# Gated linear attention and a rational MLP on one core: one activation table set, head pairs padded to 64 rows, x kept on chip, MLP steps 2048 wide

## The chip, the cores and the metric

The program runs on one core of one Trainium2 chip. The metric is the device time of one execution in microseconds (us). Engines are named as in the profile: PE is TensorE (PEld its weight loads), DVE VectorE, ACT ScalarE, POOL GpSimd, SP the queue that issues most of the DMAs.

## What is computed

Four batches, 8 heads, 768 steps, head dimension 48; then an MLP over the 3072 tokens with 384 inputs, 2048 hidden units and 384 outputs. Inputs are float32, the output is float32.

```python
f = 1.0 / (1.0 + np.exp(-f_logit))
for t in range(S):
    state = f[:, :, t, :, None] * state + np.einsum('bhd,bhe->bhde', k[:, :, t], v[:, :, t])
    y[:, :, t] = np.einsum('bhd,bhde->bhe', q[:, :, t], state)
x = y.transpose(0, 2, 1, 3).reshape(B * S, H * D)
h = x @ w_in
P = a[0] + a[1] * h + a[2] * h**2 + a[3] * h**3
Q = 1.0 + abs(b[0]) * abs(h) + abs(b[1]) * h**2
out = (P / (Q + 1e-06)) @ w_out
```

## The kernel before

The 768 steps are cut into NC = 6 chunks of C = 128. For each chunk the attention is done in two head groups of four heads, each tile holding 4 heads x 4 batches x 48 = 768 columns on 128 partitions (the steps). ACT takes the log of the gate in two steps, `sig` (Sigmoid, L113) and `lsig` (Ln, L115); PE sums it along the chunk with a triangular matrix (`csT`, L119); ACT takes exp of that sum and of its negative (L123, L125); DVE scales q (L128), POOL scales k (L130). Then, head by head: 8 transposes into `psB` (L139, L141) and two DVE copies out; scores `sc_ps` and their masking on DVE (L160, L165); `y_ps`, for each batch one matmul with the values and one with the running state (L169, L173); ACT copies `y_ps` out and SP writes it to a DRAM tensor `xT_bridge` (L179); the state is updated (L184 to L192).

The MLP of the chunk reads `xT_bridge` back (`xc`), so that its 512 tokens lie in columns. It goes through KF = 16 tiles of 128 hidden units, each 512 wide: three matmuls (`h_ps`, L203), a DVE copy to bf16 (`hb`, L207), then a chain of steps over DVE, ACT and POOL. The division is exp(-ln(Q)): `lnQ` (L226) and `Qinv` (L228) on ACT. The product goes into `gall`; when all 16 tiles are there, four groups of 16 matmuls of 384 columns each (`o_ps`, L233), one for each batch, give the output, which ACT copies out (L237).

The order on each engine is not written by hand: a scheduler interleaves the independent work of the next chunk's attention with the MLP of this one, within the limits of the pools' buffers (most PSUM pools have one buffer).

## Time and profile before

| what | value |
|---|---|
| median of 3 runs | 821.11 us (818.91 to 821.45) |
| the profiled execution's span, first to last instruction | 820.2 us |
| that execution's own time beside its span | not given apart; the median of the runs is 0.9 us above this span |
| ACT busy | 629.0 us, 77% |
| PE busy, DVE busy, POOL busy | 424.6, 386.7, 160.4 us |

The busy share is an average over stages with different limits. The timeline shows when each instruction began and how long it took; two instructions that follow each other on one engine can overlap a little, so their starts are closer than their durations. "granted clock" is PE's clock in shares of 2.4 GHz.

### The profile page before, as it was taken

To read this page: it belongs to the slowest core of one execution; us is meant where nothing else is said; L and a number is where in the kernel's file an instruction comes from. 1 tells how busy PE (TensorE), PEld (TensorE's weight loads), DVE (VectorE), ACT (ScalarE), POOL (GpSimd) and SP (SyncE) were. 2 spreads that over 40 slices of the span, in tenths; PEclk is the share of its full clock that TensorE was granted. 3 is DMA by queue.
4 is the path that set the end of the run, shared out by engine and by line. 5 is a ranking of instruction groups with operands and counts; after the bars stand their busy time and mean duration, and the time that the engine had idled before them with its cause. 6 is when DMAs were issued, how large, how long until landed. Compare 5 with 4: busy or idle time off the path is not lost. (4 is left out here: it accounts for less than half of the span.)

```text
span 820.2 us, 6861 instructions
## 1 busy us (share of the span) xinstructions
PE 424.6 (52%) x2052; PEld 185.2 (23%) x2052; DVE 386.7 (47%) x838; ACT 629.0 (77%) x780; POOL 160.4 (20%) x174
## 2 busy tenths in 40 slices
PE   0198743339923528954527843336964335643325
PEld 0055310015500104511104510003620002300002
DVE  0054554642646642665652545553555543255550
ACT  0577599994699993699993399995169996199992
POOL 3233211310312210223210221131012220021120
PEclk9999999999555557655557555556655555655557
DMA  9997530205601401412101300002100000100001
GB/s 160 152 126 86 97 58 0 13 5 125 90 0 20 49 2 36 64 24 26 26 2 38 36 9 0 0 0 34 43 14 1 0 0 19 42 0 0 0 0 40
DMA packets 127110, 29.55 MB, mean 36 GB/s; under 512 B 121569, under 2 KB 126689, under 8 KB 127073
## 3 DMA queue, kind: packets, MB, share of 16 engines
...
q14 instruction: 22, 0.17, 0.1%
...
## 5 line engine op out<-in xcount | busy, mean ns | idle before, releaser
L233 PE MATMUL o_ps<-w_out_sb,gall 128*128 128x384 bf16 x384 | 109.9, 409 | 214.2 <-DVE gall L229 211.9
L203 PE MATMUL h_ps<-xc,w_in_sb 128*128 128x512 bf16 x288 | 139.4, 612 | 98.7 <-DVE hb L207 92.5
L216 POOL TENSOR_SCALAR pB<-hb,a_sb 128x512 bf16<-128x512 bf16 x96 | 97.6, 1017 | 424.9 <-DVE hb L207 409.1
L229 DVE TENSOR_TENSOR gall<-Pp,Qinv 128x512 bf16<-128x512 bf16 x96 | 44.4, 463 | 178.2 <-ACT Qinv L228 178.2
L226 ACT ACT_TABLE_LOAD x95 | 121.9, 1283 | 1.7
L233 PEld LDWEIGHTS <-gall 128*128 128x128 bf16 x384 | 40.9, 109 | 315.9 <-DVE gall L229 286.2
L228 ACT ACT_TABLE_LOAD x85 | 109.1, 1283 | 1.5
L223 DVE SCALAR_TENSOR_TENSOR u<-h,babs,habs 128x512 bf16<-128x512 bf16 x96 | 73.0, 761 | 34.4 <-ACT habs L211 34.2
L178 ACT CAST y_sb<-y_ps 48x512 bf16<-48x512 f32 x48 | 27.7, 576 | 67.7 <-PE y_ps L173 65.3
L207 DVE CAST hb<-h_ps 128x512 bf16<-128x512 f32 x96 | 65.8, 686 | 25.2 <-PE h_ps L203 25.1
L213 ACT ACTIVATE pA<-hb,a_sb 128x512 bf16<-128x512 bf16 x96 | 77.0, 802 | 0.0
L211 ACT ACTIVATE habs<-hb,babs 128x512 bf16<-128x512 bf16 x96 | 68.1, 709 | 7.2 <-DVE hb L207 7.1
L226 ACT ACTIVATE lnQ<-u,one_eps 128x512 bf16<-128x512 bf16 x96 | 69.4, 723 | 1.1
L203 PEld LDWEIGHTS <-w_in_sb 128*128 128x128 bf16 x288 | 34.5, 124 | 154.6 <-issue 152.7
L228 ACT ACTIVATE Qinv<-lnQ 128x512 bf16<-128x512 bf16 x96 | 60.5, 630 | 0.9
L237 ACT COPY o_sb<-o_ps 128x384 f32<-128x384 f32 x24 | 11.5, 479 | 64.8 <-PE o_ps L233 63.4
L107 POOL DMA_DIRECT2D vn<-in_v_dram x48 | 36.5, 775 | 122.7 <-PE y_ps L173 109.9
L169 PE MATMUL y_ps<-sc_sb,vn 128*48 128x128 bf16 x192 | 54.1, 282 | 3.8 <-DVE sc_sb L165 2.7
L173 PE MATMUL y_ps<-qt_d,state 48*48 48x128 bf16 x192 | 54.1, 282 | 0.0
L192 DVE TENSOR_TENSOR state<-stmp,alast 48x192 bf16<-48x192 f32 x48 | 21.2, 442 | 61.2 <-PE y_ps L173 61.2
L165 DVE TENSOR_TENSOR sc_sb<-sc_ps,mask 128x512 bf16<-128x512 f32 x48 | 33.0, 688 | 33.4 <-PE sc_ps L160 33.1
L219 DVE TENSOR_TENSOR t<-pA,h 128x512 bf16<-128x512 bf16 x96 | 40.3, 420 | 17.7 <-ACT pA L213 17.7
...
## 6 DMA issues: line engine op xcount, KB each, us to landing
...
```

The lines of the kernel that those rows point to most:

```text
L169: nc.tensor.matmul(y_ps[:, b * C:(b + 1) * C], vn[:, jo + b * D:jo + (b + 1) * D], sc_sb[:, b * C:(b + 1) * C], start=True, stop=False)
L173: nc.tensor.matmul(y_ps[:, b * C:(b + 1) * C], state[:, b * D:(b + 1) * D], qt_d[:, b * C:(b + 1) * C], start=False, stop=True)
L203: nc.tensor.matmul(h_ps, w_in_sb[:, kk, m * P:(m + 1) * P], xc[:, kk].rearrange("p b s -> p (b s)"), start=(kk == 0), stop=(kk == KD - 1))
L207: nc.vector.tensor_copy(hb, h_ps)
L211: nc.scalar.activation(habs, hb, AF.Abs, scale=babs[:, 0:1])
L213: nc.scalar.activation(pA, hb, AF.Identity, scale=a_sb[:, 3:4], bias=a_sb[:, 2:3])
L216: nc.gpsimd.tensor_scalar(pB, hb, a_sb[:, 1:2], a_sb[:, 0:1], op0=ALU.mult, op1=ALU.add)
L223: nc.vector.scalar_tensor_tensor(u, h2, babs[:, 1:2], habs, op0=ALU.mult, op1=ALU.add)
L226: nc.scalar.activation(lnQ, u, AF.Ln, bias=one_eps)
L228: nc.scalar.activation(Qinv, lnQ, AF.Exp, scale=-1.0)
L229: nc.vector.tensor_mul(gall[:, m, :], Pp, Qinv)
L233: nc.tensor.matmul(o_ps, gall[:, mm, sub * C:(sub + 1) * C], w_out_sb[:, mm, :], start=(mm == 0), stop=(mm == KF - 1))
```

## The change

The kernel is written anew around the same chunks of 128 steps.

- One activation table set is loaded at the start (L45). The gate's log becomes ln(1 + exp(-f)), so that all functions on ACT are Exp, Ln, Abs and copies.
- A unit of attention is now (chunk c, batch pair u): two batches, all 8 heads, 768 columns. Twelve units. Heads lie in pairs, each padded from 48 to 64, so that one transpose turns two heads (16 transposes of 128 x 128 a unit, L151) and the state of two heads lies on 128 partitions. The zeros of the padding are written once into three rotating buffers (L60 to L66). POOL computes nothing; it only issues the loads of v and the weights.
- y comes out with steps on partitions and is transposed on PE into `xT` in SBUF (L219 to L225). There is no DRAM bridge and no read back.
- The MLP goes in 4 groups of 4 hidden tiles, each step 2048 wide. ACT copies the matmul result to bf16 (`hy`, two pieces of 1024, L240); |h| is a bitwise AND on DVE (`z`); the polynomial is evaluated on DVE in bf16 by five `tensor_scalar` steps (TENSOR_SCALAR, one tensor input; L243, L245, L253, L255, L257) and four products of two tensors (L246, L254, L256, L258); ACT keeps Ln (`lq`) and Exp (`qi`).
- Loads run three units ahead; the first unit's loads stand ahead of the weights.
- PSUM: `ps2` and `ps1`, one buffer each, are shared by tag: `cs`, `sc` and `y` take turns in one, `tp`, `sv` and `xps` in the other. `hp` has two buffers, `op` one.

```diff
...
+    nc.scalar.preload_act_table_set("natural_log_exp_and_others")
...
+    for i in range(NQK):
+        t = consts.tile([C, UB, 2, H, 64], BF16, name=f"qkp{i}")
+        nc.vector.memset(t.rearrange("p a b c d -> p (a b c d)").bitcast(F32), 0.0)
+        qkp.append(t)
+        t = consts.tile([C, UB, H, 64], BF16, name=f"lsp{i}")
+        nc.vector.memset(t.rearrange("p b c d -> p (b c d)").bitcast(F32), 0.0)
+        lsp.append(t)
...
+    def load(c, u):
+        t0 = c * C
+        fn = ld.tile([C, UB, H, D], F32, name="fn")
+        kn = ld.tile([C, UB, H, D], F32, name="kn")
+        qn = ld.tile([C, UB, H, D], F32, name="qn")
+        vn = ld.tile([C, UB, H, D], BF16, name="vn")
+        for j in range(UB):
+            b = u * UB + j
+            for dst, src, eng in ((fn, f_logit, nc.sync), (kn, k, nc.sync),
+                                  (qn, q, nc.sync), (vn, v, nc.gpsimd)):
+                eng.dma_start(out=dst[:, j],
+                              in_=src[b, :, t0:t0 + C, :].rearrange("h t d -> t h d"))
+        loaded[c, u] = (fn, kn, qn, vn)
...
-            sig = sb.tile([C, GD], F32, tag="sig")
-            nc.scalar.activation(sig, fn, AF.Sigmoid)
-            lsig = bf.tile([C, GD], BF16, tag="lsig")
-            nc.scalar.activation(lsig, sig, AF.Ln)
...
-            AT = hsb.tile([C, GD], F32, tag="AT")
-            nc.scalar.activation(AT, csT, AF.Exp, scale=1.0)
-            AinvT = hsb.tile([C, GD], F32, tag="AinvT")
-            nc.scalar.activation(AinvT, csT, AF.Exp, scale=-1.0)
-            qt_n = bf.tile([C, GD], BF16, tag="qt_n")
-            nc.vector.tensor_mul(qt_n, qn, AT)
-            kt_n = bf.tile([C, GD], BF16, tag="kt_n")
-            nc.gpsimd.tensor_mul(kt_n, kn, AinvT)
...
+        ef = at.tile([C, UB, H, D], F32, name="ef")
+        nc.scalar.activation(ef.rearrange(fl), fn.rearrange(fl), AF.Exp, scale=-1.0)
+        nc.scalar.activation(ls[:, :, :, 0:D], ef, AF.Ln, bias=1.0)
+        cs = ps2.tile([C, 2, 512], F32, name="cs", tag="w2")
+        for j in range(UB):
+            nc.tensor.matmul(cs[:, j, 0:DM].rearrange("p (h d) -> p h d", h=H), U, ls[:, j, :, 0:D],
+                             start=True, stop=True)
+        A = at.tile([C, UB, H, D], F32, name="A")
+        Ai = at.tile([C, UB, H, D], F32, name="Ai")
+        nc.scalar.activation(A.rearrange("p b h d -> p b (h d)"), cs[:, :, 0:DM], AF.Exp, scale=-1.0)
+        nc.scalar.activation(Ai.rearrange("p b h d -> p b (h d)"), cs[:, :, 0:DM], AF.Exp, scale=1.0)
+        nc.vector.tensor_mul(qk[:, :, 0, :, 0:D], qn, A)
+        nc.vector.tensor_mul(qk[:, :, 1, :, 0:D], kn, Ai)
...
+        for j in range(UB):
+            tp = ps1.tile([P, 2, HP, C], BF16, name="tp", tag="w1")
+            for i in range(2):
+                for p in range(HP):
+                    nc.tensor.transpose(tp[:, i, p, :],
+                                        qk[:, j, i, 2 * p:2 * p + 2, :].rearrange("t h d -> t (h d)"),
+                                        ident)
+            t = at.tile([P, 2, HP, C], BF16, name="qkT", bufs=4)
+            nc.scalar.copy(t.rearrange("p a b c -> p (a b c)"), tp.rearrange("p a b c -> p (a b c)"))
...
+            sv = ps1.tile([P, 512], F32, name="sv", tag="w1")
+            svv = sv[:, 0:UB * HP * D].rearrange("p (b h e) -> p b h e", b=UB, h=HP)
+            al = sv[:, 448:448 + UB * HP]
+            for j in range(UB):
+                for p in range(HP):
+                    nc.tensor.matmul(al[:, j * HP + p:j * HP + p + 1],
+                                     ls[:, j, 2 * p:2 * p + 2, :].rearrange("t h d -> t (h d)"),
+                                     ones, start=True, stop=True)
+                    for i in range(2):
+                        h = 2 * p + i
+                        nc.tensor.matmul(svv[64 * i:64 * i + 64, j, p, :],
+                                         qk[:, j, 1, h, :], vn[:, j, h, :],
+                                         start=True, stop=True)
+        scm = []
+        for j in range(UB):
+            sc = ps2.tile([C, 2, HP, C], F32, name="sc", tag="w2")
+            for p in range(HP):
+                for i in range(2):
+                    r = slice(64 * i, 64 * i + D)
+                    nc.tensor.matmul(sc[:, i, p, :], qkT[j][r, 1, p, :], qkT[j][r, 0, p, :],
+                                     start=True, stop=True)
+            m = at.tile([C, 2 * HP, C], BF16, name="scm", bufs=4)
+            mb = bass.AP(tensor=mask.tensor, offset=mask.offset,
+                         ap=[mask.ap[0], [0, 2 * HP], mask.ap[1]])
+            nc.vector.tensor_mul(m, sc.rearrange("s i p t -> s (i p) t"), mb)
...
-                nc.scalar.copy(y_sb, y_ps)
-                nc.sync.dma_start(
-                    out=xT[h * D:(h + 1) * D, :].rearrange("d (b s) -> d b s", b=B)[:, :, t0:t0 + C],
-                    in_=y_sb.rearrange("d (b c) -> d b c", b=B))
...
+        y = ps2.tile([C, 2, 512], F32, name="y", tag="w2")
+        yv = y[:, :, 0:UB * HP * D].rearrange("t i (b p e) -> t i b p e", b=UB, p=HP)
+        for j in range(UB):
+            for p in range(HP):
+                for i in range(2):
+                    h = 2 * p + i
+                    nc.tensor.matmul(yv[:, i, j, p, :], scm[j][:, i * HP + p, :], vn[:, j, h, :],
+                                     start=True, stop=(c == 0))
+                    if c > 0:
+                        r = slice(64 * i, 64 * i + D)
+                        nc.tensor.matmul(yv[:, i, j, p, :], qkT[j][r, 0, p, :], st[r, j, p, :],
+                                         start=False, stop=True)
+        ysb = at.tile([C, UB, HP, 2, D], BF16, name="ysb")
+        for i in range(2):
+            nc.scalar.copy(ysb[:, :, :, i, :].rearrange("t b p e -> t (b p) e"),
+                           yv[:, i].rearrange("t b p e -> t (b p) e"))
+        if c < NC - 1:
+            alast = at.tile([P, UB * HP], F32, name="alast")
+            nc.scalar.activation(alast, al, AF.Exp, scale=-1.0)
+            ab = bass.AP(tensor=alast.tensor, offset=alast.offset,
+                         ap=[alast.ap[0], alast.ap[1], [0, D]])
+            stv = st.rearrange("p b h e -> p (b h) e")
+            svf = svv.rearrange("p b h e -> p (b h) e")
+            if c == 0:
+                nc.vector.tensor_mul(stv, svf, ab)
+            else:
+                stmp = at.tile([P, UB * HP, D], F32, name="stmp")
+                nc.vector.tensor_add(stmp, svf, stv)
+                nc.vector.tensor_mul(stv, stmp, ab)
+        for j in range(UB):
+            b = u * UB + j
+            xps = ps1.tile([P, KD, C], BF16, name="xps", tag="w1")
+            yf = ysb[:, j].rearrange("t p i e -> t (p i e)")
+            for kk in range(KD):
+                nc.tensor.transpose(xps[:, kk, :], yf[:, kk * P:(kk + 1) * P], ident)
+            nc.scalar.copy(xT[:, :, b * C:(b + 1) * C], xps)
...
-        xc = msb.tile([P, KD, B, C], BF16, tag="xc")
-        for kk in range(KD):
-            nc.sync.dma_start(out=xc[:, kk],
-                              in_=xT.rearrange("d (b s) -> d b s", b=B)[kk * P:(kk + 1) * P, :, t0:t0 + C])
...
-            nc.vector.tensor_copy(hb, h_ps)
-            h2 = msb.tile([P, NT], BF16, tag="h2")
-            nc.vector.tensor_mul(h2, hb, hb)
-            habs = msb.tile([P, NT], BF16, tag="habs")
-            nc.scalar.activation(habs, hb, AF.Abs, scale=babs[:, 0:1])
-            pA = msb.tile([P, NT], BF16, tag="pA")
-            nc.scalar.activation(pA, hb, AF.Identity, scale=a_sb[:, 3:4],
-                                 bias=a_sb[:, 2:3])
-            pB = msb.tile([P, NT], BF16, tag="pB")
-            nc.gpsimd.tensor_scalar(pB, hb, a_sb[:, 1:2], a_sb[:, 0:1],
-                                    op0=ALU.mult, op1=ALU.add)
-            t1 = msb.tile([P, NT], BF16, tag="t1")
-            nc.vector.tensor_mul(t1, pA, h2)
-            Pp = msb.tile([P, NT], BF16, tag="Pp")
-            nc.vector.tensor_add(Pp, t1, pB)
-            u = msb.tile([P, NT], BF16, tag="u")
-            nc.vector.scalar_tensor_tensor(u, h2, babs[:, 1:2], habs,
-                                           op0=ALU.mult, op1=ALU.add)
-            lnQ = msb.tile([P, NT], BF16, tag="lnQ")
-            nc.scalar.activation(lnQ, u, AF.Ln, bias=one_eps)
-            Qinv = msb.tile([P, NT], BF16, tag="Qinv")
-            nc.scalar.activation(Qinv, lnQ, AF.Exp, scale=-1.0)
-            nc.vector.tensor_mul(gall[:, m, :], Pp, Qinv)
...
+        gall = gp.tile([P, KF, NT], BF16, name="gall")
+        W = G * NT
+        for g in range(KF // G):
+            y = ms.tile([P, W], BF16, name="hy")
+            for hh in range(G // 2):
+                hp = psh.tile([P, 2, NT], F32, name="hp")
+                for e in range(2):
+                    m = g * G + hh * 2 + e
+                    for kk in range(KD):
+                        nc.tensor.matmul(hp[:, e, :], w_in_sb[:, kk, m * P:(m + 1) * P], xT[:, kk, :],
+                                         start=(kk == 0), stop=(kk == KD - 1))
+                nc.scalar.copy(y[:, hh * 2 * NT:(hh + 1) * 2 * NT], hp.rearrange("p a n -> p (a n)"))
+            z = ms.tile([P, W], BF16, name="z", bufs=1)
+            nc.vector.tensor_scalar(z.bitcast(U16), y.bitcast(U16), 0x7FFF, None, op0=ALU.bitwise_and)
+            w = ms.tile([P, W], BF16, name="w")
+            nc.vector.tensor_scalar(w, z, babs[:, 1:2], babs[:, 0:1], op0=ALU.mult, op1=ALU.add)
+            nc.vector.tensor_mul(w, w, z)
+            lq = ms.tile([P, W], F32, name="lq", bufs=1)
+            nc.scalar.activation(lq, w, AF.Ln, bias=one_eps)
+            qi = ms.tile([P, W], BF16, name="qi")
+            nc.scalar.activation(qi, lq, AF.Exp, scale=-1.0)
+            t = ms.tile([P, W], BF16, name="t")
+            nc.vector.tensor_scalar(t, y, a_sb[:, 3:4], a_sb[:, 2:3], op0=ALU.mult, op1=ALU.add)
+            nc.vector.tensor_mul(t, t, y)
+            nc.vector.tensor_scalar(t, t, a_sb[:, 1:2], None, op0=ALU.add)
+            nc.vector.tensor_mul(t, t, y)
+            nc.vector.tensor_scalar(t, t, a_sb[:, 0:1], None, op0=ALU.add)
+            nc.vector.tensor_mul(gall[:, g * G:(g + 1) * G, :].rearrange("p a n -> p (a n)"), t, qi)
+        for b in range(B):
+            op = pso.tile([P, DM], F32, name="op")
+            for mm in range(KF):
+                nc.tensor.matmul(op, gall[:, mm, b * C:(b + 1) * C], w_out_sb[:, mm, :],
+                                 start=(mm == 0), stop=(mm == KF - 1))
+            osb = ms.tile([P, DM], F32, name="osb")
+            nc.scalar.copy(osb, op)
+            nc.sync.dma_start(out=out[b * S + c * C:b * S + (c + 1) * C, :], in_=osb)
...
+    AHEAD = 3
+    for x in order[:1]:
+        load(*x)
+    load_weights()
+    for x in order[1:AHEAD]:
+        load(*x)
+    nxt = AHEAD
+    for c in range(NC):
+        xT = xp.tile([P, KD, NT], BF16, name="xT")
+        for u in range(NU):
+            if nxt < len(order):
+                load(*order[nxt])
+                nxt += 1
+            attention(c, u, xT)
+        mlp(c, xT)
```

ACT, in the MLP of a chunk before: `lnQ` and `Qinv` are Ln and Exp of one tile of 512 columns, `habs` and `pA` belong to its neighbours.

```order
L228 ACT_TABLE_LOAD
L228 ACTIVATE Qinv<-lnQ 128x512
L226 ACT_TABLE_LOAD
L226 ACTIVATE lnQ<-u,one_eps 128x512
L211 ACTIVATE habs<-hb,babs 128x512
L228 ACT_TABLE_LOAD
L228 ACTIVATE Qinv<-lnQ 128x512
L213 ACTIVATE pA<-hb,a_sb 128x512
```

ACT, in the MLP of chunk 1 after the change: `hy` are the copies out of `hp`, `lq` and `qi` Ln and Exp of a group, and `qkT` the copy of the next chunk's transposed q and k.

```order
L240 CAST hy<-hp 128x1024 [waits PE_49] x2
L240 CAST hy<-hp 128x1024 [waits DVE_49,PE_49]
L240 CAST hy<-hp 128x1024 [waits PE_49]
L248 ACTIVATE lq<-w,one_eps 128x2048 [waits DVE_49]
L155 COPY qkT<-tp 128x1024 [waits PE_49]
L250 ACTIVATE qi<-lq 128x2048 [waits Activation_49]
L240 CAST hy<-hp 128x1024 [waits DVE_49]
L248 ACTIVATE lq<-w,one_eps 128x2048 [waits DVE_49,Activation_49]
L240 CAST hy<-hp 128x1024
L250 ACTIVATE qi<-lq 128x2048 [waits Activation_49]
```

The table loads are gone from between Ln and Exp, the copies of the second group stand ahead of the first group's Ln, and a copy that waits for PE (`qkT`) stands between the first group's Ln and Exp.

DVE, in the same place after the change: the first 12 steps of the MLP of chunk 1, groups one and two in turn.

```order
L243 TENSOR_SCALAR z<-hy 128x2048
L253 TENSOR_SCALAR t<-hy,a_sb 128x2048
L245 TENSOR_SCALAR w<-z,babs 128x2048
L254 TENSOR_TENSOR t<-t,hy 128x2048
L246 TENSOR_TENSOR w<-w,z 128x2048
L255 TENSOR_SCALAR t<-t,a_sb 128x2048
L243 TENSOR_SCALAR z<-hy 128x2048
L256 TENSOR_TENSOR t<-t,hy 128x2048
L245 TENSOR_SCALAR w<-z,babs 128x2048
L257 TENSOR_SCALAR t<-t,a_sb 128x2048
L246 TENSOR_TENSOR w<-w,z 128x2048
L258 TENSOR_TENSOR gall<-t,qi 128x2048
```

Before, DVE took seven steps of 512 for each of the 16 tiles, with ACT's `habs` and `pA` and POOL's `pB` between them; now nine steps of 2048 for each of 4 groups, and only `hy` and `qi` come from another engine.

DVE, at the end of the same MLP: the last group's steps and those of the next chunk's first attention unit (`scm`, `stmp`, `state`), up to the second unit's q.

```order
L258 TENSOR_TENSOR gall<-t,qi 128x2048 [waits DVE_49,Activation_49]
L254 TENSOR_TENSOR t<-t,hy 128x2048 [waits DVE_49]
L185 TENSOR_TENSOR scm<-sc,mask 128x1024 [waits PE_49]
L255 TENSOR_SCALAR t<-t,a_sb 128x2048 [waits DVE_49]
L216 TENSOR_TENSOR stmp<-sv,state_85 128x384 [waits Activation_49]
L256 TENSOR_TENSOR t<-t,hy 128x2048 [waits DVE_49]
L217 TENSOR_TENSOR state_85<-stmp,alast 128x384 [waits DVE_49,PE_49]
L257 TENSOR_SCALAR t<-t,a_sb 128x2048 [waits DVE_49]
L258 TENSOR_TENSOR gall<-t,qi 128x2048 [waits DVE_49,Activation_49]
L143 TENSOR_TENSOR qkp_81<-qn,A 128x2x8x48 [waits DMAHW5_49,DMAHW2_49,Activation_49]
```

Before, the state of one head was updated between tiles of 512. Now the state update of a unit, which waits for PE to have read the old state in the `y` matmuls, stands ahead of the last two steps of the MLP's last group.

## Rows read from the trace of the kernel before

**Rows 1.** The page, busy time, share of the span and instructions of the engines.

```profile
PE 424.6 (52%) x2052; PEld 185.2 (23%) x2052; DVE 386.7 (47%) x838; ACT 629.0 (77%) x780; POOL 160.4 (20%) x174
```

**Rows 2.** The page, the chain of work that ended last, by engine.

```profile
ACT 20%; PE 7%; issue 1%; DVE 1%; DMA 1%; ACTq 0%; SPq 0%
```

**Rows 3.** Timeline in one MLP: start, duration, engine, line, instruction [idle before].

```profile
640.50 0.63 ACT L228 ACTIVATE Qinv<-lnQ 128x512 bf16<-128x512 bf16 x1
641.04 0.71 ACT L211 ACTIVATE habs<-hb,babs 128x512 bf16<-128x512 bf16 x1
641.16 0.43 DVE L229 TENSOR_TENSOR gall<-Pp,Qinv 128x512 bf16<-128x512 bf16 x1 [2.61 <-ACT Qinv L228]
641.51 0.42 DVE L221 TENSOR_TENSOR Pp<-t,pB 128x512 bf16<-128x512 bf16 x1
641.84 0.42 DVE L209 TENSOR_TENSOR h<-hb 128x512 bf16<-128x512 bf16 x1
...
642.47 1.28 ACT L226 ACT_TABLE_LOAD   x1
...
642.91 1.44 PE L203 MATMUL h_ps<-xc,w_in_sb 128*128 128x512 bf16 x3 [0.76 <-DVE hb L207]
...
645.80 0.63 ACT L228 ACTIVATE Qinv<-lnQ 128x512 bf16<-128x512 bf16 x1
```

**Rows 4.** Groups by line and form, ACT: busy us, mean ns | idle before.

```profile
L226 ACT ACT_TABLE_LOAD x95 | 121.9, 1283 | 1.7
...
L228 ACT ACT_TABLE_LOAD x85 | 109.1, 1283 | 1.5
...
L226 ACT ACTIVATE lnQ<-u,one_eps 128x512 bf16<-128x512 bf16 x96 | 69.4, 723 | 1.1
...
L237 ACT COPY o_sb<-o_ps 128x384 f32<-128x384 f32 x24 | 11.5, 479 | 64.8 <-PE o_ps L233 63.4 <-issue 1.4
...
L113 ACT ACTIVATE sig<-fn 128x768 f32<-128x768 f32 x12 | 10.1, 844 | 0.6 <-DMA fn<-in_f_logit_dram 0.5
...
L123 ACT ACTIVATE AT<-csT 128x768 f32<-128x768 f32 x12 | 9.7, 806 | 1.2 <-PE csT L119 1.2
```

**Rows 5.** Groups by line and form, DVE.

```profile
L223 DVE SCALAR_TENSOR_TENSOR u<-h,babs,habs 128x512 bf16<-128x512 bf16 x96 | 73.0, 761 | 34.4 <-ACT habs L211 34.2
...
L209 DVE TENSOR_TENSOR h<-hb 128x512 bf16<-128x512 bf16 x96 | 41.4, 431 | 0.1
...
L165 DVE TENSOR_TENSOR sc_sb<-sc_ps,mask 128x512 bf16<-128x512 f32 x48 | 33.0, 688 | 33.4 <-PE sc_ps L160 33.1
...
L144 DVE COPY qt_d<-psB 48x512 bf16<-48x512 bf16 x48 | 19.8, 413 | 13.2 <-PE psB L141 13.1
...
L128 DVE TENSOR_TENSOR qt_n<-qn,AT 128x768 bf16<-128x768 f32 x12 | 11.3, 945 | 33.6 <-ACT AT L123 33.5
```

**Rows 6.** Timeline of PE: two of the attention's matmuls, two output bursts.

```profile
42.75 0.30 PE L173 MATMUL y_ps<-qt_d,state 48*48 48x128 bf16 x1
...
42.98 0.30 PE L169 MATMUL y_ps<-sc_sb,vn 128*48 128x128 bf16 x1
...
563.57 4.81 PE L233 MATMUL o_ps<-w_out_sb,gall 128*128 128x384 bf16 x16
...
569.58 2.77 PE L233 MATMUL o_ps<-w_out_sb,gall 128*128 128x384 bf16 x16
```

**Rows 7.** Two stretches: busy us (count) of PE, PEld, DVE, ACT, POOL; granted clock; DMA.

```profile
570.00:575.00 5.00, 5.00 (x37) 2.97 (x36) 1.35 (x3) 0.48 (x1) 2.56 (x4) 1.00 1.04 115
585.00:590.00 5.00, 5.00 (x34) 2.97 (x33) 2.56 (x7) 0.65 (x2) 0.00 (x0) 0.50 0.18 41
```

**Rows 8.** One line, L203, in the first 220 us: duration ns min/median/max.

```profile
L203 PE MATMUL h_ps<-xc,w_in_sb x53: 390/631/634, 68.9 to 220.0; 128*128 128x512 bf16 x53
```

**Rows 9.** Timeline of ACT: the first attention work.

```profile
28.80 1.28 ACT L113 ACT_TABLE_LOAD   x1 [24.81 <-DMA fn<-in_f_logit_dram]
```

More of the change, by code (lines that the diff above doesn't have):

```diff
@@ L10 @@
 BF16 = mybir.dt.bfloat16
+U16 = mybir.dt.uint16
 AF = mybir.ActivationFunctionType
 ALU = mybir.AluOpType
+PSUM = bass.MemoryType.PSUM
 @with_exitstack
@@ L49 @@
     make_upper_triangular(nc, U, 1.0, diag=True)
[L50 to L53 removed]
+    ident = consts.tile([C, C], BF16, name="ident")
     make_identity(nc, ident)
[L55 to L60 removed]
@@ L61 @@
-    w_out_sb = w_pool.tile_from(moe_w_out.rearrange("(ko ki) n -> ki ko n", ki=P),
-                                dtype=BF16, name="w_out_sb")
-    a_sb = w_pool.tile([P, 4], F32)
+    ones = consts.tile([C, 1], BF16, name="ones")
+    nc.vector.memset(ones, 1.0)
+    one_eps = consts.tile([P, 1], F32, name="one_eps")
+    nc.vector.memset(one_eps, 1.0 + 1e-6)
+    NQK = 3
+    qkp = []
+    lsp = []
+    for i in range(NQK):
[5 more added lines that the diff above has]
+        lsp.append(t)
@@ L64 @@
+    states = []
+    for u in range(B // UB):
+        st = consts.tile([P, UB, HP, D], BF16, name=f"state{u}")
+        states.append(st)
+    w_pool = ctx.enter_context(tc.tile_pool(name="w_pool", bufs=1))
+    a_sb = w_pool.tile([P, 4], F32, name="a_sb")
     nc.sync.dma_start(out=a_sb, in_=bass.AP(tensor=moe_a.tensor, offset=moe_a.offset,
                                             ap=[[0, P]] + list(moe_a.ap)))
-    b_sb = w_pool.tile([P, 2], F32)
+    b_sb = w_pool.tile([P, 2], F32, name="b_sb")
@@ new lines @@
+    ld = ctx.enter_context(tc.tile_pool(name="ld", bufs=3))
+    at = ctx.enter_context(tc.tile_pool(name="at", bufs=2))
+    xp = ctx.enter_context(tc.tile_pool(name="xp", bufs=2))
+    gp = ctx.enter_context(tc.tile_pool(name="gp", bufs=2))
+    ms = ctx.enter_context(tc.tile_pool(name="ms", bufs=2))
+    ps2 = ctx.enter_context(tc.tile_pool(name="ps2", bufs=1, space=PSUM))
+    ps1 = ctx.enter_context(tc.tile_pool(name="ps1", bufs=1, space=PSUM))
+    psh = ctx.enter_context(tc.tile_pool(name="psh", bufs=2, space=PSUM))
@@ new lines @@
+    pso = ctx.enter_context(tc.tile_pool(name="pso", bufs=1, space=PSUM))
+    mask = consts.tile([C, C], F32, name="mask")
+    make_upper_triangular(nc, mask, 1.0, diag=True)
+    loaded = {}
+    def load(c, u):
+        t0 = c * C
+        fn = ld.tile([C, UB, H, D], F32, name="fn")
[9 more added lines that the diff above has]
+        loaded[c, u] = (fn, kn, qn, vn)
@@ new lines, in mlp @@
+    def mlp(c, xT):
+        w_in_sb, w_out_sb = w_sb["in"], w_sb["out"]
+        gall = gp.tile([P, KF, NT], BF16, name="gall")
[28 more added lines that the diff above has]
+            op = pso.tile([P, DM], F32, name="op")
@@ L232 @@
             for mm in range(KF):
-                nc.tensor.matmul(o_ps, gall[:, mm, sub * C:(sub + 1) * C],
-                                 w_out_sb[:, mm, :],
+                nc.tensor.matmul(op, gall[:, mm, b * C:(b + 1) * C], w_out_sb[:, mm, :],
                                  start=(mm == 0), stop=(mm == KF - 1))
-            o_sb = msb.tile([P, d_model], F32, tag="o_sb")
-            nc.scalar.copy(o_sb, o_ps)
-            nc.sync.dma_start(out=out[sub * S + t0: sub * S + t0 + C, :], in_=o_sb)
+            osb = ms.tile([P, DM], F32, name="osb")
@@ new lines, in mlp @@
+            nc.scalar.copy(osb, op)
+            nc.sync.dma_start(out=out[b * S + c * C:b * S + (c + 1) * C, :], in_=osb)
+    NU = B // UB
+    order = [(c, u) for c in range(NC) for u in range(NU)]
+    AHEAD = 3
[13 more added lines that the diff above has]
+        mlp(c, xT)
```

150 lines of the change are left out of this document (27 added, 123 removed).

## Prediction

> **What bounds the kernel now.** I begin with the busy shares: ACT 77%, DVE 47% [rows 1]. The chain of waits says the same: of what it follows back from the end, ACT has 20% of the span and PE 7%, DMA 1% [rows 2]. The timeline shows why. From one `Qinv` to the next, 640.50 to 645.80, one tile of 512 takes 5.30 us, and ACT works through it without a pause, while DVE waits 2.61 us for `Qinv` and PE 0.76 us for a buffer [rows 3]. Two of the pieces on ACT are table loads of 1.28 us. The groups count 95 of them at L226 and 85 at L228, 231 us of pure switching between Ln and Exp [rows 4]. So a gain begins at ACT, and it ends where the next engine becomes the bound.
>
> **What each engine does afterwards.** Prices come from the same rows.
>
> ACT: 630 ns for 512 columns [rows 3] and 844 for 768 [rows 4] give 0.83 ns a column and 0.2 us fixed; from PSUM 806 for 768; `lnQ` with its pointer bias costs 0.09 us more than `Qinv` [rows 3, 4]. Two neighbours start 0.54 us apart where one lasts 0.63 [rows 3], so 0.09 overlaps. An MLP group then costs two copies of 1024 at 1.02, `lq` of 2048 at 2.0 and `qi` at 1.9: 5.9 us, 24 times 142 us. An attention unit costs four functions of 768 (3.3), two `qkT` copies of 1024 (2.0), four copies of 384 at 0.48 and small things: 7.5 us, 12 times 89. With 24 output copies at 0.48 ACT comes to 243 us, from 629.
>
> DVE: products of two bf16 tensors of 512 start 0.33 to 0.35 us apart [rows 3], which is 256 cycles of 0.96 GHz and 0.07 us: 2 columns a cycle, so 1.14 us for 2048. The new `tensor_scalar` steps, one bf16 tensor each, have no row on DVE. The rows bound them. A product takes in 8 bytes a cycle, two tensors at 2 columns of bf16; the float32 product of 768 in 945 ns [rows 5] also takes in 8 bytes a cycle. If one tensor alone can use that intake, `tensor_scalar` runs 4 columns a cycle, 0.60 us for 2048. Against it, the copy of one bf16 tensor from PSUM, 413 ns for 512, is no faster than a product, and the three-operand step takes 761 ns [rows 5], 1 column a cycle. So the ends are 0.60, 1.14 and 2.2 us, and below 0.60 nothing, since no row takes in more than 8 bytes. I take 0.60, because the two SBUF products of different width agree on the intake and the copy comes from PSUM. The page "VectorE: DVE Perf Modes" of the Trainium skill, section "The perf-mode tier table", puts `tensor_scalar` on bf16 in SBUF at four times the base rate, 693 ns for 2048; with starts at that distance the total below would be about 11 us longer (0.09 us, 120 times), and no run of before shows it. A group is 5 x 0.60 + 4 x 1.14 = 7.6 us, 24 times 181. A unit adds two masks of 1024 from PSUM (688 ns for 512 [rows 5], so 1.22), two products of 768, and `stmp` and the state at some 0.5 each: 5.3 us, 12 times 63. DVE comes to about 245 us.
>
> PE: a 512-column matmul takes 0.43 us at 1.2 GHz (three in 1.44 [rows 3]), and a burst of 16 x 384 columns 4.81 us at the start of a dense stretch and 2.77 later [rows 6]. The granted clock falls in with this: 1.00 in the stretch with the fast burst, 0.50 fifteen us later among small attention matmuls, though PE was busy all the time [rows 7]. In the first 220 us the page's clock digits are 9, but the median `h_ps` lasted 631 ns [rows 8], the slow level; there I trust the durations. The `y` matmuls start 0.23 us apart [rows 6] where 128 columns need 0.11 at 1.2 GHz, so 0.12 more for a change between 128 and 48 rows; with 48 columns I take 0.17. All 672 large matmuls together are 239 us slow and about 125 fast; a unit's small ones, 22 transposes, 16 scores, 24 for the state, 32 for `y`, 11.5 slow and some 8 fast, 12 times.
>
> No engine is full: ACT 243, DVE 245, PE between 220 and 375 with its clock. What decides is how they take turns, so I add along the path of one chunk.
>
> **One chunk.** (a) From `xT` complete: 12 matmuls for the first group, 5.4 us, and its last copy, 1.0: 6.4. (b) DVE, four groups: 30.2. ACT follows: a group's Ln, Exp, two copies are 5.9 us less overlaps, under DVE's 7.6. (c) On DVE in between, the next chunk's first unit: two masks, `stmp`, state: 3.2. (d) The state update stands in DVE's order ahead of the last two steps of group four; it waits for 32 `y` matmuls after the second mask, 5.4 us, covered by 2.2 us of other steps. Stall 3.6, with 1.4 for the first groups' waits on `qi` and `hy` (`qkT` stands between Ln and Exp). Sum 45 us. (e) Then DVE has nearly nothing. PE finishes the first output (1.5), its copy frees the single `op` (0.5), second burst 4.8, copy 0.5, third 2.8, copy 0.5, fourth 2.8: 13.4. The next chunk's second unit is threaded through: 24 state matmuls 1.5, mask 1.4, scores 0.7, mask 1.2, 32 `y` matmuls 5.5, two copies 0.9, transposes and `xT` copies 2.4: 13.6. Sum 27. A chunk is 72 us. This counts hardly anything for handing over; rows show 0.03 us from `Qinv`'s end to `gall` [rows 3], and I add 0.08 for each of 25 hand-overs on the path, 2 us: 74.
>
> **The ends.** The first attention now waits for DMA until 28.8 us [rows 9], for 12 loads of four batches of 128 x 48 float32, 1.2 MB. The first unit now needs the same bytes of q, k and f, with the weights issued at about the same place, so I keep 29. Two units alone, 16 us each, and (a), 6.4: the first MLP step at 67. The last chunk has no attention in it: 31 on DVE, then outputs and the last store, 19: 50. The sum is 67 + 5 x 74 + 52 = 489. The median is 0.9 us above the profiled span, so 490.
>
> **What goes at no cost.** The bridge through DRAM goes (its waits had 1% of the chain [rows 2]); its place is taken by transposes and copies in (e). Loads now number fewer and larger and run three units ahead: a unit has some 35 us, and moved in 29 us while the weights moved too [rows 9]. Without that cover each late unit would cost its delay.
>
> **Rivals.**
> - PE stays at 2.4 GHz once the denser kernel runs: (a) falls by 2.6, the second burst by 2.0, the rest by 2: chunk 67, start 62; with the last chunk 442. For it, 24 matmuls of 512 columns in a row at each MLP's start. Against it, the clock fell in stretches of small matmuls that kept PE busy [rows 7]. Chance 0.12.
> - PE stays at 1.2 GHz: the third and fourth bursts cost 2 more each, and matmuls of groups two and three come so late that `qkT`, and behind it `qi`, holds DVE by 4, with some 3 for transposes, scores and `hy` that wait behind them; chunk 85, in all 550. The same time, 547, comes from `tensor_scalar` at 2 columns a cycle: 0.54 x 5 x 24 = 65 us more, some 8 of it in stalls that exist. Together 0.16.
> - `tensor_scalar` at 1 column a cycle, as the three-operand step [rows 5]: 1.6 x 20 = 32 us a chunk more, part of it hidden: 667. Chance 0.08.
> - The change doesn't remove the loads: that can't be, since ACT's order has one at its head and no other.
> - Slower than before: loads become the bound. They are still runs of 192 bytes, and a unit's loads behind the weights took 29 us [rows 9]. At that rate 12 units need 348 us, hidden under 490. It would decide only if a unit took 68 us, 821 over 12, more than twice the contended rate. Chance 0.02.
>
> My forecast, 470 to 525, has 0.55; the remaining 0.07 lies between 525 and 640, for hand-overs dearer than taken. The likeliest time is 490. The range 438 to 565 reaches over both clock rivals and the 2-column case and leaves out about 0.15. Faster by over 0.3% (about what a measurement of this kernel tells from no change): 0.97, within 0.3% 0.01, slower 0.02.
>
> **What would show it.** One table load on ACT and some 245 us busy; `tensor_scalar` of 2048 near 0.7 us long; DVE 4 to 5 us idle before the state of the first unit, waiting for `y`, and over 10 us idle once a chunk during the outputs; the first Exp near 25 us; output bursts of 4.8 then 2.8. The forecast is wrong if DVE's steps are longer, if PE's clock holds one level, or if chunks take other than 74 us.

## The result

The changed kernel takes 471.78 us (median of 4 runs, 469.32 to 472.01) where the kernel before took 820.16 in the same comparison: a ratio of 0.5745, interval 0.573 to 0.5761. The forecast was 490, its own range 470 to 525, the wide range 438 to 565; the time lies near the lower edge of the former. The profiled execution has a span of 469.9 us, and the profile times below are from it.

The page of the changed kernel, busy times and the chain of work that ended last:

```profile
PE 293.4 (62%) x1744; PEld 157.4 (33%) x1744; DVE 257.8 (55%) x290; ACT 231.3 (49%) x252; POOL 24.9 (5%) x36
...
PE 44%; DVE 29%; ACT 15%; SPq 6%; issue 4%; DMA 2%; DVEq 0%; ACTq 0%
```

Beside [rows 1, 2]: ACT fell from 629 to 231 us, and no engine is busy for two thirds of the span. The chain now goes through three engines by turns. The groups by line and form (busy us, mean ns, then idle time ahead of them and its causes) give the price of each step:

```profile
L238 PE MATMUL hp<-xT,w_in_sb 128*128 128x512 bf16 x288 | 92.1, 490 | 19.0 <-ACT hy L240 14.1 <-ACT xT L225 4.9
...
L248 ACT ACTIVATE lq<-w,one_eps 128x2048 f32<-128x2048 bf16 x24 | 48.1, 2005 | 28.1 <-DVE w L246 28.1
...
L246 DVE TENSOR_TENSOR w<-w,z 128x2048 bf16<-128x2048 bf16 x24 | 29.2, 1218 | 0.0
...
L253 DVE TENSOR_SCALAR t<-hy,a_sb 128x2048 bf16<-128x2048 bf16 x24 | 19.4, 807 | 0.0
...
L255 DVE TENSOR_SCALAR t<-t,a_sb 128x2048 bf16<-128x2048 bf16 x24 | 17.9, 747 | 0.0
...
L243 DVE TENSOR_SCALAR z<-hy 128x2048 uint16<-128x2048 uint16 x24 | 16.5, 689 | 41.6 <-ACT hy L240 41.6
...
L45 ACT ACT_TABLE_LOAD x1 | 1.3, 1283 | 0.7 <-PEq L299 0.7
```

One table load is left of the 180 in [rows 4] and the rest of that kind. The `tensor_scalar` steps are the fastest of the prediction's three cases, for which it had 0.60, 1.14 and 2.2 us from start to start: they last 689 ns with no pointer (a [P, 1] operand such as a column of `a_sb`), 747 with one, 807 with two. The Trainium skill, page "VectorE: DVE Perf Modes", section "The perf-mode tier table", gives 693 ns for 2048 columns. The trace agrees for the step without pointers.

One chunk on DVE (start, duration, [idle before, and who ended it]) shows the turns:

```profile
139.19 0.69 DVE L243 TENSOR_SCALAR z<-hy 128x2048 uint16<-128x2048 uint16 x1 [4.58 <-ACT hy L240]
...
161.85 0.69 DVE L243 TENSOR_SCALAR z<-hy 128x2048 uint16<-128x2048 uint16 x1 [1.29 <-ACT hy L240]
...
176.03 0.56 DVE L217 TENSOR_TENSOR state<-stmp,alast 128x384 bf16<-128x384 f32 x1 [2.78 <-PE y L198]
...
177.62 1.23 DVE L258 TENSOR_TENSOR gall<-t,qi 128x2048 bf16<-128x2048 bf16 x1
...
193.30 1.22 DVE L185 TENSOR_TENSOR scm<-sc,mask 128x1024 bf16<-128x1024 f32 x1 [12.29 <-PE sc L180]
...
201.28 0.56 DVE L217 TENSOR_TENSOR state<-stmp,alast 128x384 bf16<-128x384 f32 x1 [5.04 <-PE y L198]
...
210.86 0.69 DVE L243 TENSOR_SCALAR z<-hy 128x2048 uint16<-128x2048 uint16 x1 [4.59 <-ACT hy L240]
```

From the first `z` to the end of the last `gall` (178.85) DVE has work for 39.7 us with two short waits. Then it idles most of 32 us, while PE makes the outputs and the second unit of the next chunk. PE in that stretch:

```profile
175.62 0.22 PE L194 MATMUL y<-vn,scm 128*128 128x48 bf16 x1
175.77 0.22 PE L198 MATMUL y<-state,qkT 48*128 48x48 bf16 x1
176.94 0.50 PE L224 MATMUL xps<-ident,ysb 128*128 128x128 bf16 x3 [0.95 <-ACT ysb L202]
...
178.91 1.46 PE L262 MATMUL op<-w_out_sb,gall 128*128 128x384 bf16 x4 [0.41 <-DVE gall L258]
...
184.88 2.76 PE L262 MATMUL op<-w_out_sb,gall 128*128 128x384 bf16 x16 [0.34 <-ACT osb L265]
...
188.26 2.76 PE L262 MATMUL op<-w_out_sb,gall 128*128 128x384 bf16 x16
...
204.61 6.68 PE L238 MATMUL hp<-xT,w_in_sb 128*128 128x512 bf16 x19 [0.86 <-ACT xT L225]
```

The `y` matmuls start 0.155 us apart, 32 of them in 4.95 us. The output bursts are at the fast level of [rows 6], and the first matmuls of the next MLP, after 14 us of small ones with pauses between them, again take 0.43 us each (the first 12 take 5.2 us).

### The profile page after: what moved, and what is told of

It reads as the page before. It is cut to its first block, busy times and chain, and to the rows that moved or that the text cites. A ratio compares the mean times of both kernels' runs of the same rounds, so it can differ in the third digit from the quotient of the medians.

```text
span 469.9 us, 4398 instructions
## 1 busy us (share of the span) xinstructions
PE 293.4 (62%) x1744; PEld 157.4 (33%) x1744; DVE 257.8 (55%) x290; ACT 231.3 (49%) x252; POOL 24.9 (5%) x36
## 4 chain that ended last, share of the span: by engine, by line
PE 44%; DVE 29%; ACT 15%; SPq 6%; issue 4%; DMA 2%; DVEq 0%; ACTq 0%
PE op L262 14%; PE hp L238 11%; PE y L194 6%; SPq L107 6%; PE y L198 5%; DVE scm L185 5%; ACT hy L240 4%; DVE gall L258 4%; DVE t L254 4%; DVE w L246 3%; ACT lq L248 3%; DVE t L256 3%; PE sv L170 2%; DVE w L245 2%; DVE t L257 2%
## 5 line engine op out<-in xcount | busy, mean ns | idle before, releaser
L262 PE MATMUL op<-w_out_sb,gall 128*128 128x384 bf16 x384 | 88.7, 387 | 69.0 <-DVE gall L258 64.9
L238 PE MATMUL hp<-xT,w_in_sb 128*128 128x512 bf16 x288 | 92.1, 490 | 19.0 <-ACT hy L240 14.1
L248 ACT ACTIVATE lq<-w,one_eps 128x2048 f32<-128x2048 bf16 x24 | 48.1, 2005 | 28.1 <-DVE w L246 28.1
L240 ACT CAST hy<-hp 128x1024 bf16<-128x1024 f32 x48 | 48.1, 1007 | 24.7 <-PE hp L238 23.6
L185 DVE TENSOR_TENSOR scm<-sc,mask 128x1024 bf16<-128x1024 f32 x24 | 29.3, 1220 | 53.9 <-PE sc L180 53.8
L250 ACT ACTIVATE qi<-lq 128x2048 bf16<-128x2048 f32 x24 | 46.0, 1915 | 0.3
L194 PE MATMUL y<-vn,scm 128*128 128x48 bf16 x192 | 36.9, 220 | 13.5 <-DVE scm L185 13.5
L202 ACT CAST ysb<-y 128x384 bf16<-128x384 f32 x24 | 10.3, 482 | 69.8 <-PE y L198 66.2
L243 DVE TENSOR_SCALAR z<-hy 128x2048 uint16<-128x2048 uint16 x24 | 16.5, 689 | 41.6 <-ACT hy L240 41.6
L198 PE MATMUL y<-state,qkT 48*128 48x48 bf16 x160 | 35.0, 219 | 0.0
L151 PE MATMUL tp<-ident,qkp 128*128 128x128 bf16 x192 | 18.8, 242 | 25.5 <-ACT qkT L155 16.1
L258 DVE TENSOR_TENSOR gall<-t,qi 128x2048 bf16<-128x2048 bf16 x24 | 29.3, 1220 | 0.6
L256 DVE TENSOR_TENSOR t<-t,hy 128x2048 bf16<-128x2048 bf16 x24 | 29.2, 1218 | 0.1
L254 DVE TENSOR_TENSOR t<-t,hy 128x2048 bf16<-128x2048 bf16 x24 | 29.2, 1217 | 0.0
L246 DVE TENSOR_TENSOR w<-w,z 128x2048 bf16<-128x2048 bf16 x24 | 29.2, 1218 | 0.0
L151 PEld LDWEIGHTS <-qkp 128*128 128x128 bf16 x192 | 14.6, 108 | 33.0 <-issue 17.1
```

The lines of the kernel that those rows point to most:

```text
L185: nc.vector.tensor_mul(m, sc.rearrange("s i p t -> s (i p) t"), mb)
L194: nc.tensor.matmul(yv[:, i, j, p, :], scm[j][:, i * HP + p, :], vn[:, j, h, :], start=True, stop=(c == 0))
L198: nc.tensor.matmul(yv[:, i, j, p, :], qkT[j][r, 0, p, :], st[r, j, p, :], start=False, stop=True)
L238: nc.tensor.matmul(hp[:, e, :], w_in_sb[:, kk, m * P:(m + 1) * P], xT[:, kk, :], start=(kk == 0), stop=(kk == KD - 1))
L240: nc.scalar.copy(y[:, hh * 2 * NT:(hh + 1) * 2 * NT], hp.rearrange("p a n -> p (a n)"))
L246: nc.vector.tensor_mul(w, w, z)
```

## The experiments

All are variants of the changed kernel (471.78 us) unless another is named. Each was timed against the kernel before on its own chip, which took 819.5 to 820.5 us there. The times given are medians of 4 runs.

**Only one part: the table set in the kernel before.**

```diff
+    nc.scalar.preload_act_table_set("natural_log_exp_and_others")
-            nc.scalar.activation(sig, fn, AF.Sigmoid)
+            nc.scalar.activation(sig, fn, AF.Exp, scale=-1.0)
-            nc.scalar.activation(lsig, sig, AF.Ln)
+            nc.scalar.activation(lsig, sig, AF.Ln, bias=1.0)
```

(and the signs of the three Exp that follow).

> The kernel before with one part of the change alone: one table set at the head, and the log-sigmoid by Exp and Ln. 226 loads of 1.283 us go, 290 us of ACT's 629. Theory (ACT was the bound of the tile loop, then DVE at some 3 us a tile of 512 and the attention in between): 560 us (530 to 600), three quarters of the whole gain. Rival (the chain of one tile through DVE, ACT, DVE with two buffers holds it above 4 us a tile): 650 to 700.

596.27 us, ratio 0.7263 (0.725 to 0.7277). The table set alone brings 224 of the 348 us. The first and the last `Qinv` of one MLP, and what PE, PEld, DVE, ACT and POOL did between them (busy us and count, then granted clock and DMA):

```profile
454.99 0.62 ACT L230 ACTIVATE Qinv<-lnQ 128x512 bf16<-128x512 bf16 x1
500.06 0.63 ACT L230 ACTIVATE Qinv<-lnQ 128x512 bf16<-128x512 bf16 x1
455.00:500.00 45.00, 25.88 (x59) 6.26 (x59) 43.77 (x91) 39.26 (x61) 19.25 (x14) 0.50 0.01 2
```

The same stretch in the kernel before:

```profile
608.00:687.00 79.00, 28.59 (x70) 6.80 (x70) 40.76 (x91) 78.01 (x91) 16.16 (x14) 0.50 0.00 0
```

The tiles come unevenly, 1.7 to 5.2 us apart; over all six MLPs a tile takes 3.05 us on average where it took 5.42. ACT was busy for 78.0 of 79 us, and now DVE is for 43.8 of 45. So the theory's 3 us a tile with DVE as the next bound holds, and the rival's 4 us and more are out. These stretches give 214 of the 225 us between the two spans. The time is 36 us above the theory's all the same; these lie outside the stretches, and no run separates them. Of the other 124 us of the change only the width of the steps is undone by itself, below; the bridge, the pairing of heads and POOL's work have no run of their own.

**One part undone: the table loads.** The line that chooses the set is left out, so that Ln and Exp come from sets of their own.

```diff
-    nc.scalar.preload_act_table_set("natural_log_exp_and_others")
```

> Without the one table set chosen at the head the program has 65 table loads of 1.283 us, 83 us more on ACT, in the rebuilt kernel otherwise unchanged. Theory (no engine is full, and ACT idles 13 of 38 us in the elementwise phase): most hides, Ln and Exp of a group come 2.6 later, some 5 us a chunk on the path: 500 us (490 to 520). Rival (ACT is still the bound): the whole 83, 555 us. Second rival (all of it hidden): 472 to 478.

504.14 us, ratio 0.6148 (0.6132 to 0.6163). The two largest groups of loads, and what they add:

```profile
L248 ACT ACT_TABLE_LOAD x24 | 30.8, 1283 | 0.4
L246 ACT ACT_TABLE_LOAD x20 | 25.7, 1283 | 6.8 <-DVE w L244 6.5
```

ACT went from 231 to 316 us busy, the time by 32. The first theory stands: only 32 of the 84 us show in the time, so some 50 fell where ACT would have idled. There are fewer loads to undo here, 64 against 226 in the kernel before, but each also counts for less: 0.5 us of time here, 1.0 us where ACT was the bound.

**One part undone: the width.**

```diff
-    G = 4
+    G = 1
-    psh = ctx.enter_context(tc.tile_pool(name="psh", bufs=2, space=PSUM))
+    psh = ctx.enter_context(tc.tile_pool(name="psh", bufs=4, space=PSUM))
-                hp = psh.tile([P, 2, NT], F32, name="hp")
+                hp = psh.tile([P, 1, NT], F32, name="hp")
```

> The elementwise steps 512 wide instead of 2048, four times as many, hp of one bank in four slots. Theory (in the stretch of the elementwise steps DVE sets the pace, and a narrow step pays its fixed cost again): 4 x (5 x 0.20 + 4 x 0.34) = 9.4 us of DVE for what takes 7.9, ACT some 6.8 for 5.7, 24 times 1.5 = 36 us: 507 us (495 to 520). Rival (the first step can start after 3 matmuls and one copy instead of 12 and two, and the engines hand over in smaller pieces, some 4 us a chunk back): 480 to 490.

526.79 us, ratio 0.6425 (0.641 to 0.6441). The direction was that of the theory, the size was not. The groups show the term:

```profile
L245 DVE TENSOR_SCALAR w<-z,babs 128x512 bf16<-128x512 bf16 x96 | 38.7, 403 | 0.0
...
L255 DVE TENSOR_SCALAR t<-t,a_sb 128x512 bf16<-128x512 bf16 x96 | 32.9, 343 | 0.1
...
L243 DVE TENSOR_SCALAR z<-hy 128x512 uint16<-128x512 uint16 x96 | 27.2, 283 | 14.0 <-ACT hy L240 14.0
```

I had taken 0.20 us from start to start for each. That is right only for the step without a pointer; the steps with one last 60 ns longer, those with two 120, at this width as at the other. The steps differ in more than pointers (none: one bitwise operation on uint16; one: one addition; two: a multiplication and an addition), and no run separates pointers from operations. DVE's busy time rose from 258 to 328 us.

**The stall of step (d).** Two state tiles by turns:

```diff
-        st = states[u]
+        st, sn = states[u][c % 2], states[u][(c + 1) % 2]
-                nc.vector.tensor_mul(stv, stmp, ab)
+                nc.vector.tensor_mul(snv, stmp, ab)
```

> Two state tiles by turns, so that the state update no longer waits for the y matmuls that read the old one. Theory of the prediction's step (d) (the stall stands on the path): 2.8 us less in each of four chunks, 461 us. Rival (PE is the one that is late there: y ends 3 us before the output burst in any case, with transposes and cs between): the wait on DVE goes and the time stays within 2 us of 472.

471.03 us, ratio 0.5749 (0.5727 to 0.5772): no difference that can be told. The rival was right. The wait is gone from DVE, and here is what was late in its place:

```profile
171.42 0.56 DVE L217 TENSOR_TENSOR state<-stmp,alast 128x384 bf16<-128x384 f32 x1
171.89 0.75 DVE L257 TENSOR_SCALAR t<-t,a_sb 128x2048 bf16<-128x2048 bf16 x1
172.75 1.23 DVE L258 TENSOR_TENSOR gall<-t,qi 128x2048 bf16<-128x2048 bf16 x1
177.23 0.96 DVE L142 TENSOR_TENSOR qkp<-qn,A 128x768 bf16<-128x768 f32 x1 [3.25 <-ACT A L140]
```

PE in the same stretch has the outputs' start at the end:

```profile
174.04 0.22 PE L197 MATMUL y<-state,qkT 48*128 48x48 bf16 x1
175.21 0.50 PE L224 MATMUL xps<-ident,ysb 128*128 128x128 bf16 x3 [0.95 <-ACT ysb L201]
...
176.55 1.49 PE L262 MATMUL op<-w_out_sb,gall 128*128 128x384 bf16 x4
```

`gall` is done at 174.0, but PE has the `y` block until 174.3 and then transposes, and the output burst starts at 176.55. Counted from the chunk's first `z` that is 39.0 us, where it was 39.7 with the stall. DVE had waited for work that PE had to finish in any case.

**The y block itself.** The state is kept with zeros in the rows of the other head, so both kinds of matmul take 128 rows:

```diff
-                        r = slice(64 * i, 64 * i + D)
-                        nc.tensor.matmul(yv[:, i, j, p, :], qkT[j][r, 0, p, :], st[r, j, p, :],
+                        nc.tensor.matmul(yv[:, i, j, p, :], qkT[j][:, 0, p, :], st[:, j, p, i, :],
```

> The state is kept padded with zeros, so that the y matmuls with the state take 128 rows like those with the mask, at the same columns and count; the state update writes two halves, two more DVE steps a unit. Theory (a change between 128 and 48 rows costs about 0.10 us each time): a y block of 32 falls from 4.95 us to about 1.6, the pitch of 0.05 that the 16 of chunk 0 have. Ten units have it, all on the path: 33 us less, 5 given back on DVE, 444 us (435 to 455). Rival (every one of these matmuls loads its own weights, 0.11 us, and that sets the pitch): the block stays near 5 us, and the time at 472 to 480.

445.64 us, ratio 0.5432 (0.5419 to 0.5446), as the theory said.

```profile
165.09 0.21 PE L198 MATMUL y<-state,qkT 128*128 128x48 bf16 x1
165.13 0.21 PE L195 MATMUL y<-vn,scm 128*128 128x48 bf16 x1
165.17 0.21 PE L198 MATMUL y<-state,qkT 128*128 128x48 bf16 x1
```

The starts are 0.04 us apart instead of 0.155, with as many matmuls and weight loads as before. It is not the 48 rows by themselves. In the changed kernel the scores, all with 48 rows, and the `y` of chunk 0, all with 128, run without such gaps:

```profile
42.58 0.80 PE L194 MATMUL y<-vn,scm 128*128 128x48 bf16 x16 [1.45 <-DVE scm L185]
194.58 0.40 PE L180 MATMUL sc<-qkT 48*128 48x128 bf16 x8 [1.32 <-DVE scm L185]
```

That is 0.05 us from start to start in both. So 0.115 us of each `y` matmul was the change between 128 and 48 rows; both blocks compared, 0.155 and 0.04, are at a granted clock of 0.50. The Trainium skill says, on the page "TensorEngine Tiling (Array Packing)", section "Key Properties", that a change of tiling mode drains the engine. If matmuls of 48 rows count as another mode than those of 128, which no run shows, this run agrees with it and gives the price.

**Two slots for the output sums.**

```diff
-            op = pso.tile([P, DM], F32, name="op")
+            op = psh.tile([P, 2, NT], F32, name="op", tag="hp")[:, 0, 0:DM]
```

> The output sums take two of the slots of hp instead of the one slot of op. Theory (each burst waits for the copy of the one before): gaps of 0.56 and 0.62 us between bursts go, with those of the first and last some 2 us a chunk, 460 us (455 to 464). Rival (the slots are those of the next chunk's hp, or other work fills the gaps): 470 to 480.

454.62 us, ratio 0.5541 (0.5526 to 0.5557), 17 us less where 12 were expected.

```profile
155.15 5.52 PE L261 MATMUL op<-w_out_sb,gall 128*128 128x384 bf16 x16 [1.36 <-ACT hy L239]
164.87 2.74 PE L261 MATMUL op<-w_out_sb,gall 128*128 128x384 bf16 x8 [4.19 <-DVE gall L257]
174.60 8.38 PE L261 MATMUL op<-w_out_sb,gall 128*128 128x384 bf16 x40 [0.42 <-DVE gall L257]
```

The outputs that are left after the last `gall` are one block of 40 matmuls in 8.4 us, where it took 12.1 us from 178.91 to the end of the last burst. The waits for the copies are gone, and the transposes that had slipped in between the bursts come after the block. The expectation had left out the other half: with a second slot the second output starts early too, so 24 of the 64 matmuls are done beside the elementwise steps, and 40 are left instead of 52.

**Another order.** Both units of chunk c+1 are written ahead of the MLP of chunk c:

```diff
+    units(0)
     for c in range(NC):
-        xT = xp.tile([P, KD, NT], BF16, name="xT")
...
-        mlp(c, xT)
+        if c + 1 < NC:
+            units(c + 1)
+        mlp(c, xTs.pop(c))
```

> Both attention units of the next chunk are written ahead of a chunk's MLP, so they come first where both could go. Theory (no engine is full, ACT 231, DVE 258 and PE 293 of 470; a chunk's 72 us are turns, of which 25.7 us from the last gall to xT hold the second unit while DVE idles 19): the second unit runs beside the elementwise steps, a chunk costs some 13 us less, five times, 405 us (380 to 430). Rival (the units stand in the way of the MLP on the same three in-order engines, as much as they did behind it): 460 to 485.

> The order of the run before and the state padded to 128 rows together. Theory (PE's time for the small matmuls is still on the path): the gain of 26 us of the padding stays, 380 us (355 to 400). Rival (with the units beside DVE's steps the y matmuls are hidden): within 5 us of the run before.

376.57 us, ratio 0.4584 (0.4561 to 0.4607), and with the padded state 355.46, ratio 0.4336 (0.4326 to 0.4346). The direction is that of both theories. The first gained 28 us more than the 405 expected and lies under its range; the padding gave 21 us where 26 were to stay. Two things were left out. One is that the next MLP no longer waits. In the kernel with the order alone, the first `z` of chunk 1 stands ahead of the last `gall` of chunk 0:

```profile
120.25 0.68 DVE L243 TENSOR_SCALAR z<-hy 128x2048 uint16<-128x2048 uint16 x1
...
122.24 1.21 DVE L258 TENSOR_TENSOR gall<-t,qi 128x2048 bf16<-128x2048 bf16 x1
```

In the changed kernel it came 32 us after it. So not only the second unit, but the outputs and the first matmuls of the next MLP too run beside the elementwise steps. The other is PE's clock. The first matmuls of an MLP in the changed kernel, by a window (length, PE busy and count, granted clock, DMA share, GB/s):

```profile
204.60:209.80 5.20, 5.19 (x13) 0.53 0.93 141
```

The first 12 in the kernel of 355 us:

```profile
201.80:204.50 2.70, 2.70 (x12) 1.00 0.44 23
```

The same work takes half the time: one is at 1.2 GHz nearly throughout, the other at 2.4. In the first, PE comes from 14 us of small matmuls with pauses; in the second, matmuls of outputs stand among them, and the padded state shortens the `y` blocks. With the order alone the granted clock was 0.80 on average from 67 to 350 us, against 0.69 from 67 to 400 us in the changed kernel, and over the whole span PE's busy time fell from 293 to 269 us. How the additional 28 us divide between the two, no run separates.

**What DVE costs.** One more copy of the first DVE step per group, once in the changed kernel and once in the one of 355 us:

```diff
+            zz = ms.tile([P, W], BF16, name="zz", bufs=1)
+            nc.vector.tensor_scalar(zz.bitcast(U16), y.bitcast(U16), 0x7FFF, None, op0=ALU.bitwise_and)
```

> One more step on DVE in each of 24 groups, a copy of the first (128x2048, 0.60 us from start to start) whose result nobody reads: 14.4 us of DVE. Theory (DVE paces only the elementwise stretch, and even there 1.3 us of waiting for hy and 2.8 us for y absorb part of it): 480 us (475 to 484). Rivals: DVE paces it all, 486; DVE is hidden behind PE and ACT, 472.

> The same additional DVE step in the kernel with the units ahead and the state padded (355 us). Theory (there DVE is the bound: 268 us busy of 355, and of the 270 between its first MLP step and its last some nine tenths): nearly the whole 14.4 us appear, 369 us (366 to 372). Rival (turns are taken there as before): 358 to 363.

483.85 us (0.5903, 0.5888 to 0.5917), 12.1 more for 14.4 us of DVE; and 369.61 (0.4504, 0.4484 to 0.4524), 14.2 more. In the second nearly the whole step appears, as expected where DVE sets the pace: there it is busy for 250 of the 272.5 us between the start of the MLPs and the last `gall`. In the changed kernel the waits absorbed less than I thought, 2.3 us instead of 6: DVE is busy for only 55% of the span, but most of its elementwise time lies on the path.

**The head.** The weight loads wait for the first unit's loads:

```diff
+            nc.gpsimd.tensor_copy(t[:, 0, 0:1], qn0[:, UB - 1, 0, 0:1])
+            nc.gpsimd.dma_start(out=t, in_=src.rearrange("(ko ki) n -> ki ko n", ki=P))
```

> The two weight loads wait for the last q load of the first unit (a one-column copy into each weight tile comes ahead of it), otherwise the rebuilt kernel. Theory (the first unit's six loads end at 28.6 us because 3 MB of weights move beside them): they end near 15, and the first MLP step comes some 12 us sooner: 460 us (455 to 466). Rival (the short runs of 192 bytes set the pace of these loads, or the weights are then late for the first MLP): 470 to 482.

470.32 us, ratio 0.5733 (0.572 to 0.5745): not to be told from 471.78. But the loads did what the theory said. The first DVE step of the attention moved from 28.61 to 15.48 us. ACT, in order of time, shows where it was lost:

```profile
29.61 0.83 ACT L144 ACTIVATE Ai<-cs 128x768 f32<-128x768 f32 x1
45.06 0.84 ACT L134 ACTIVATE ef<-fn 128x768 f32<-128x768 f32 x1 [14.62 <-DMA fn<-in_f_logit_dram]
45.94 0.84 ACT L135 ACTIVATE lsp<-ef 128x768 bf16<-128x768 f32 x1
46.69 0.99 ACT L157 COPY qkT<-tp 128x1024 bf16<-128x1024 bf16 x1
```

The first Exp of the third unit stands in ACT's order ahead of the second unit's `qkT` copies, and now its load is the one that the weights delay. The first MLP step came at 64.20 instead of 67.22. By the last chunk's first step only 0.8 of these 3.0 us was left (419.37 for 420.17); no run shows what took the rest.

**All together.** To the kernel of 355 us the late weights are added, and in the last chunk the four output sums run side by side:

```diff
+            for mm in range(KF):
+                for b in range(B):
+                    nc.tensor.matmul(ops[b], gall[:, mm, b * C:(b + 1) * C], w_out_sb[:, mm, :],
```

> The units ahead, the state padded, the weights late, and in the last chunk the output sums of all four batches taken group by group in the two slots of hp, so that after the last gall only 16 matmuls and four copies are left instead of 52. Theory (each is on the path by itself: 12 us at the head, and at the end 16 x 0.17 + 4 x 0.48 instead of 14 us, some 9): 355 - 21 = 334 us (328 to 342). Rival (what the head gains is lost where the next loads are late, or DVE's order shifts): 345 to 355.

344.72 us, ratio 0.4209 (0.4197 to 0.4221), the fastest of all, 10.7 less than 355.46; I had expected 21, and at most 342 us. The head gave 2.9 us (first MLP step at 65.51 after 68.39), for the reason above. From the end of the last `gall` to the end of the span it was 16.7 us and is 10.3, so the tail gave 6.4 of the 9. The trace shows two things in the way:

```profile
328.08 7.88 PE L272 MATMUL op<-w_out_sb,gall 128*128 128x384 bf16 x32 [7.44 <-DVE gall L264]
...
338.15 0.98 ACT L276 COPY osb<-op 128x384 f32<-128x384 f32 x2 [1.61 <-DMA out_dram<-osb]
```

The third group's 16 matmuls, at 0.32 us each, are still running when the last `gall` is done at 332.07, so that the last 16 begin at 333.2; and the last two copies wait 1.6 us for the stores of the first two.

## Why the prediction was right

- **What bounded the kernel before** was ACT with its table loads: the one table set alone, in the old kernel, takes a tile from 5.42 to 3.05 us on average and brings 224 us. The prediction's 5.30 us a tile was one pair of `Qinv`, close to that average.
- **The prices.** ACT 231 us for 243, DVE 258 for 245. I took 0.60 us for every `tensor_scalar`; the starts are 0.60, 0.66 and 0.72 us apart for steps with none, one and two pointers, so a DVE group is 7.9 us and not 7.6. The 2-column and 1-column cases fell. (A tile before took six DVE steps, not seven as the section on the change says; no sum used that.)
- **The sum.** The start was 67.2 us (67 forecast). A chunk from `z` to `z` was 71.7 to 72.0 for the first four (74): 6.3 from `xT` to the first `z` (6.4), 39.7 on DVE (38.4), 25.7 from the last `gall` to the next `xT` (27, and 2 for handing over). The end was 49.7; the prediction works it out as 50, but adds 52. That DVE's stretch came out so close is in part luck: the four groups together were dearer by 1.4 us, and the stall of (d) shorter by 0.8.
- **What was mis-sized.** The 19 us between the sum of 489 and the span of 469.9 are in three terms. Four chunks were some 2 us shorter each, which is what I had added for handing over. The fifth took 65.8 instead of 74: its units are those of the last chunk, which keep no state, so the state's steps and their stalls fall away; I had added five equal chunks. The end was 2 us shorter. To the span the prediction added 0.9 us for the execution's time; it is 2.0 (471.93 for 469.9).
- **A step that was wrong though the sum was not:** the stall of (d) was there, 2.78 us for the 3.6 forecast, but not on the path. Without it the time stayed. What stood there was the `y` block on PE and the transposes behind it, and the `y` blocks of all units together are worth 26 us over the kernel.
- **The clock** changed level as forecast: fast in the output bursts, slow in the first matmuls of an MLP. (In the first MLP too, by durations: its first 12 matmuls take 5.3 us, though the granted clock stands at 1.00 there; [rows 8] have the same contradiction.) In the second burst it rose sooner than I took it (3.4 us for 4.8).
- **Two signs** came otherwise than named: the first Exp began at 20.1 us, not near 25 (the unit still waited until 28.6, for q), and DVE idled 2.8 us ahead of the first unit's state, not 4 to 5.
- **The loads** were no bound. But the 29 us for the first unit were not the price of its 1.2 MB alone; with the weights held back it took half of that.
